# Two rounds of H3 and S4D long convolutions: rounded angles on ScalarE and VectorE, a folded factor 2 dt, and other DRAM layouts for spectra and y

## The chip, the core and the metric

The kernel runs on one core of one Trainium2 chip. Times are device microseconds of one launch. The engines are named as in the profile: PE is TensorE (PEld its weight loads), DVE is VectorE, ACT is ScalarE, POOL is GpSimd, SP is SyncE, which issues nearly all DMAs here. Each engine works through its own instructions in the order in which the program holds them; an instruction that waits holds back everything behind it on that engine.

## The reference, cut to what matters

```python
def _A_ref(q, k, v, shift_k, ssm_k, ssm_D):        # q is the normed x
    kv = k_shift * v                               # k_shift: short causal convolution of k
    y = irfft(rfft(kv) * rfft(ssm_k))[:S] + kv * ssm_D      # along 2048 positions, padded to 4096
    return q * y

def _B_ref(u, log_A_real, A_imag, C_real, C_imag, log_dt, D_skip):
    dt = exp(log_dt)
    A = -exp(log_A_real) + 1j * A_imag
    C = (C_real + 1j * C_imag) * dt[:, None]
    P = exp((A * dt[:, None])[:, :, None] * pos)   # 512 channels, 128 modes, 2048 positions
    K = 2.0 * einsum("dn,dnl->dl", C, P).real
    y = irfft(rfft(u) * rfft(K))[:L]
    return y + u * D_skip

x = x + _A_ref(_layernorm(x), k, v, shift_k, ssm_k, ssm_D)
x = x + _B_ref(_layernorm(x), ...)
x = x + _A_ref(_layernorm(x), k, v, shift_k, ssm_k, ssm_D)
x = x + _B_ref(_layernorm(x), ...)
```

x is 2048 x 512 in float32. A's convolution y doesn't depend on x, so it is computed once and used in both rounds. B's kernel K doesn't depend on x either.

## The kernel before, in words

**Layout.** A position is 16 times a partition number plus a row t: x is a tile of 128 partitions x 16 rows x 512 channels. A convolution along 4096 points is done by matmuls with DFT matrices in two steps, with a VectorE transpose of 32 x 32 blocks between them, for one quarter q of 128 channels at a time: `fwd_group` (matmuls into `pf` at L171, transposes into `zk` or `zu` at L191), `f2_chunk` (matmuls into `pu` at L196, eight chunks c per quarter), the product with the spectrum, the inverse matmuls into `pi` (L290), a transpose into `w` (L305) and matmuls into `po` (L311).

**Parameters.** The part behind L326 makes four numbers for each channel and mode: the rate of the angle, the phase of C, the decay, and log|C|. `split` stores them in DRAM as `rows_d`. It also makes `dt2`, which is 2 dt broadcast over partitions.

**B's kernel K.** `taps` makes it in 64 steps (16 groups gi of 32 channels, four steps k each). A step takes an exponential of the decay and log|C| (`mags`, tiles `m1`, `m2`), an angle in turns (`angles`, a matmul into the PSUM tile `pa`), cosine and sine of it (`waves`, into `tt`), products of both (`products`, into `xy` and back into `tt`), and small matmuls that sum over the modes (`contract`, into the PSUM tile `pk`). [...] Before, VectorE rounds the angle by adding and subtracting a large number, and a second matmul with minus the identity subtracts the rounded number inside PSUM:

```python
V.tensor_scalar(y, pa, MAGIC, MAGIC, op0=ALU.add, op1=ALU.subtract)      # L482
T.matmul(pa, minus, y, start=False, stop=True, skip_group_check=True)    # L483
```

ScalarE then reads `pa` three times for a step: the absolute value (L491), a sine of `pa` for the sine (L492) and a sine of the absolute value for the cosine (L493). After four steps of a group, two VectorE multiplications (L528, L529) bring `pk` times `dt2` into `ks`, which goes to DRAM (`kdram`). Exponentials and sines need different tables of ScalarE, so the twelve exponentials of two groups stand together.

**Spectra.** `spectrum_quarter` reads K (which = 1) or A's kernel (which = 0) from DRAM, transforms it, copies each chunk from PSUM to `pc` (L244) and stores that in `spec` (L245), a 256-KB chunk at a time. `convolution` loads the chunks as `kab` (L259), with one DMA for each half of the partitions. `pc` has two buffers.

**A's part.** `diagonal` computes the gated kv, A's spectrum, and `convolution(0)`, which copies its result from `po` to `ya` (L655) and stores it in `ya_d`, 16 tiles of 128 x 512. `gated_update` runs once in each round: it loads a quarter of the 16 rows of `ya_d` as `yaq` (L703; in the first round x too, at L701), forms (x + nm) * y in `ut` on one of three engines (L714, L717, L719, L720) and adds rs times that to x (L721).

**Order of the program.** `run_steps` interleaves the generators of taps (with B's spectrum at its end) and of A's part, one step to two. Within the bounds that the data set, a scheduler at build time puts the instructions of every engine in an order of its own, by times that it assumes. So a change in one place moves instructions in others. By the names, the program runs in this order: parameters, taps beside A's spectrum and gated kv, taps beside A's convolution, the first gated update beside the last taps, the norm and the end of B's spectrum, `conv_b(0)`, the second gated update, `conv_b(1)` with the stores of the result. Memory for x and for the tiles of the first gated update comes free when A's convolution is done.

Of the kernel before, what the change touches and what calls it, by code (L numbers as in the profile page):

```python
# [9 lines left out]
F32 = mybir.dt.float32  # L10
# [89 lines left out]
def kernel(ctx: ExitStack, tc: tile.TileContext, out, x_in, kv_in, ssmk_in, ssmd_in,  # L100
# [119 lines left out]
    def spectrum_quarter(which, q, src, pool, zlast, zb, tag):  # L220
# [18 lines left out]
        for c in range(NCH):  # L239
            pu, ins = f2_chunk(z, c, None, tag)  # L240
            if c == NCH - 1:
                zlast.append(ins)
            pc = pool.tile([128, CK * 128], F32, name="pc", tag="pc", bufs=2)
            S.copy(pc, pu.rearrange("p k c -> p (k c)"))  # L244
            nc.sync.dma_start(spec[which][q][c], pc)  # L245
            yield
# [3 lines left out]
    def convolution(which, pools, steps, finish, lag, ahead, nk, ns, nw, inplace, add_dve, zlast=None, late_step=None, first_b=False):  # L250
# [3 lines left out]
        def load(s):  # L254
            q, c = divmod(s, NCH)
            pool = pools["conv"]
            kab = pool.tile([128, 2, CK, 128], F32, name="kab", tag="kab", bufs=nk)
            for h in range(2):
                (G if first_b and s < GL else nc.sync).dma_start(kab[64 * h:64 * h + 64].rearrange("p r k c -> p r (k c)"),  # L259
                                  spec[which][q][c].rearrange("(r k) x -> k r x", r=2))  # L260
# [73 lines left out]
    G.memset(warm, 0.0)  # L334
    S.activation(warm, warm, AF.Exp)
    dt = gp.tile([128, 4], F32, name="dt")
    nc.sync.dma_start(dt, ldt_in)
    nc.sync.dma_start(flat(cr), cr_in)
# [7 lines left out]
    dt2 = gp.tile([128, NQ, 32], F32, name="dt2")  # L346
    halfpi = gp.tile([128, 1], F32, name="halfpi")
    G.memset(halfpi, math.pi / 2)

    minus = gp.tile([128, 128], F32R, name="minus")  # L350
    G.dma_start(minus, minus_in)

# [14 lines left out]
    across = lambda t_: t_[:, :, None].to_broadcast([128, 4, 128])  # L367
    S.activation(dt, dt, AF.Exp)
    S.activation(la, la, AF.Exp)
# [33 lines left out]
    V.scalar_tensor_tensor(t1, t3, 0.5, t1, op0=ALU.mult, op1=ALU.add)  # L403
    V.tensor_add(t2, t2, t1)

# [12 lines left out]
    S.activation(dt2, dt2, AF.Exp)  # L418
    V.tensor_scalar_mul(dt2, dt2, 2.0)
    nctx.close()  # L420
# [22 lines left out]
    rows, ms, xys, pks, angs = {}, {}, {}, {}, {}  # L443
    NXY = 2
    NM1 = 9
    NM2 = 5
# [27 lines left out]
    def angles(gi, k):  # L474
        h, s = divmod(k, 2)
        hs = slice(64 * h, 64 * h + 64)
        pa = pp.tile([128, 512], F32, name="pa", tag="pa", bufs=NPA)
        T.matmul(pa, rows[gi][hs, 0, :], tabs["tt"][hs, 8 * s:8 * s + 8, :], start=True, stop=False,
                 skip_group_check=True)

        y = wk.tile([128, 512], F32R, name="y", tag="y", bufs=2)
        V.tensor_scalar(y, pa, MAGIC, MAGIC, op0=ALU.add, op1=ALU.subtract)  # L482
        T.matmul(pa, minus, y, start=False, stop=True, skip_group_check=True)  # L483
        angs[gi, k] = pa

    def waves(gi, k):
# [4 lines left out]
        S.activation(co, rv, AF.Abs)  # L491
        for i in (S.activation(tt[:, 1, :, 1:65], rv, AF.Sin, scale=TWO_PI),  # L492
                  S.activation(co, co, AF.Sin, scale=-TWO_PI, bias=halfpi)):  # L493
            after(i, last_exp[0])
            last_sin[0] = i
# [15 lines left out]
    def contract(gi, k):  # L511
# [10 lines left out]
        if k < 3:  # L522
            return
        q, g = divmod(gi, 4)
        ks = wk.tile([128, 64, 8], F32, name="ks", tag="ks", bufs=2)
        d2 = dt2[:, q, 8 * g:8 * g + 8][:, :, None].to_broadcast([128, 8, 32])
        kv_ = ks.rearrange("p n c -> p c n")
        V.tensor_mul(kv_[:, :, 32:64], pk[:, :, 0:32], d2)  # L528
        V.tensor_mul(kv_[:, :, 31::-1], pk[:, :, 32:64], d2)  # L529
        for i4 in range(4):  # L530
# [58 lines left out]
    with ExitStack() as actx:  # L589
# [63 lines left out]
        def finish_a(q, g, po):  # L653
            ya = ap.tile([128, 512], F32, name="ya", tag="pc", bufs=2)
            S.copy(ya, po.rearrange("p t c -> p (t c)"))  # L655
            nc.sync.dma_start(ya_d[4 * q + g], ya)

# [39 lines left out]
    def gated_update(buffer, spare, rnd, load_x=False):  # L697
        yas = []
        for k in range(4):
            if load_x:  # L700
                nc.sync.dma_start(x[:, 4 * k:4 * k + 4, :], x_in[:, 4 * k:4 * k + 4, :])  # L701
            ya = buffer(k)
            nc.sync.dma_start(ya.rearrange("p g t c -> p g (t c)"),  # L703
                              ya_d[:, :, 128 * k:128 * k + 128].rearrange("g p x -> p g x"))
            yas.append(ya)
# [209 lines left out]
```

## Time and profile before

| | |
|---|---|
| median of three runs | 800.36 us (798.78 to 801.9) |
| profiled execution | 805.59 us |
| its span, first to last instruction | 803.8 us |
| mean granted clock of TensorE | 0.877 |
| busy: PE, DVE, POOL, ACT | 79%, 77%, 66%, 59% of the span |
| busy: weight loads of PE, beside its matmuls | 56% |
| moved by DMA | 135.47 MB, 169 GB/s on the mean |

The profile comes from one execution, whose time is 0.65% above the median; 1.8 us of it lie outside the span. A row of a group of instructions in it reads: source line, engine, operation, output and inputs by the program's names, shape, count, then busy time in us, mean ns of one instruction, and the idle time just before them with the instruction that ended most of it. No engine is full over the whole span, so the shares above are means over stages with different limits, and the stages have to be read one by one.

### The profile page before, as it was taken

The page shows a single profiled execution, that of the slowest core. Times are in us where ns is not written, and L with a number is a line of the kernel's source. Part 1 is how long each engine was busy: PE and PEld are TensorE (multiplying, and loading weights), DVE is VectorE, ACT ScalarE, POOL GpSimd, SP SyncE. Part 2 cuts the span into 40 slices and gives each one's busy share as a digit, 9 for nine tenths or more (in the row PEclk, how much of TensorE's full clock was granted, in tenths as well). Part 3 has the DMA queues.
Part 4 walks back from the last instruction along what each step waited for, and adds up shares of the span by engine and source line. Part 5 has one row for each costly group of instructions (what it writes and reads, how often), then busy time and mean ns, then how long its engine had stood idle before and what let it go on. Part 6 is the DMA issues. An engine that isn't in the chain of part 4 may idle for free. (4 is left out here: it accounts for less than half of the span.)

```text
span 803.8 us, 14448 instructions
## 1 busy us (share of the span) xinstructions
PE 635.2 (79%) x5064; PEld 447.3 (56%) x5064; DVE 621.3 (77%) x939; ACT 477.7 (59%) x879; POOL 533.7 (66%) x496
## 2 busy tenths in 40 slices
PE   3378696688799989999889863599789750998996
PEld 2255565356567747767556442386657620476673
DVE  7757979998967967647759499845668889878776
ACT  4035355345378875776785765649746525878573
POOL 4965778776778965838956277316665836288783
PEclk9676599868999999999899665789989995899999
DMA  9577177367477463664441593147987642068792
GB/s 326 188 247 270 40 241 254 108 200 254 146 215 203 127 182 110 182 171 123 115 131 34 174 341 105 46 129 199 233 200 183 159 103 54 1 164 223 201 252 105
DMA packets 89612, 135.47 MB, mean 169 GB/s; under 512 B 8508, under 2 KB 37700, under 8 KB 89028
## 3 DMA queue, kind: packets, MB, share of 16 engines
q1 hardware_dynamic: 88644, 132.13, 56.5%
q0 software_dynamic: 896, 2.43, 1.1%
q8 instruction: 40, 0.66, 0.4%
q14 instruction: 32, 0.26, 0.1%
HBM read 98.87 MB, written 35.65 MB: 167 GB/s over the span
## 5 line engine op out<-in xcount | busy, mean ns | idle before, releaser
L280 POOL TENSOR_TENSOR sw<-sw,kab 128x512 f32<-128x512 f32 x96 | 124.4, 1302 | 67.6 <-ACT sw L277 59.6
L196 PEld LDWEIGHTS pu<-zu,w 128*128 128x128 f32 x768 | 95.7, 193 | 52.9 <-DVE vv L278 18.6
L196 PE MATMUL pu<-zu,w 128*128 128x128 f32 x768 | 109.5, 285 | 15.1 <-DVE vv L278 12.8
L504 POOL TENSOR_TENSOR xy<-tt,m 128x512 f32<-128x512 f32 x64 | 84.9, 1327 | 53.5 <-ACT tt L493 23.8
L171 PE MATMUL pf<-kk,wz 128*128 128x256 f32 x256 | 86.3, 481 | 41.8 <-POOL kk L236 25.3
L278 DVE TENSOR_TENSOR vv<-pu,kab 128x512 f32<-128x512 f32 x96 | 64.9, 679 | 63.9 <-ACT sw L277 27.0
L290 PE MATMUL pi<-vv,mm 128*128 128x128 f32 x768 | 107.3, 285 | 3.5 <-DVE vv L278 2.6
L281 POOL TENSOR_TENSOR vv<-vv,sw 128x512 f32<-128x512 f32 x76 | 98.8, 1303 | 13.6 <-DVE vv L278 10.3
L290 PEld LDWEIGHTS pi<-vv,mm 128*128 128x128 f32 x768 | 96.5, 197 | 15.0 <-issue 9.1
L276 ACT ACTIVATE sw<-pu 64x512 f32<-64x512 f32 x96 | 57.0, 594 | 63.3 <-PE pu L196 60.8
L171 PEld LDWEIGHTS pf<-kk,wz 128*128 128x128 f32 x256 | 56.7, 237 | 62.3 <-POOL kk L236 33.3
L491 ACT ACTIVATE tt<-pa 128x512 f32<-128x512 f32 x64 | 38.3, 599 | 82.1 <-PE pa L483 72.3
L196 PE MATMUL pu<-zk,w 128*128 128x128 f32 x512 | 78.3, 307 | 6.4 <-DVE zk L191 4.2
L196 PEld LDWEIGHTS pu<-zk,w 128*128 128x128 f32 x512 | 72.7, 217 | 15.6 <-DVE zk L191 6.3
L505 DVE TENSOR_TENSOR tt<-tt,m 128x512 f32<-128x512 f32 x64 | 79.9, 1248 | 0.9 <-ACT tt L493 0.4
L244 ACT COPY pc<-pu 128x512 f32<-128x512 f32 x64 | 37.4, 591 | 57.3 <-PE pu L196 35.3
L506 DVE SCALAR_TENSOR_TENSOR xy<-tt,m 128x256 f32<-128x256 f32 x64 | 51.5, 805 | 25.7 <-ACT tt L492 15.3
L468 ACT ACTIVATE m<-pm 128x512 f32<-128x512 f32 x96 | 53.8, 604 | 22.6 <-PE pm L466 21.6
L483 PE MATMUL pa<-y,minus 128*128 128x512 f32 x64 | 37.1, 588 | 32.0 <-DVE y L482 30.5
L311 PE MATMUL po<-w,w 128*64 128x512 f32 x192 | 55.4, 655 | 7.3 <-DVE w L305 7.0
L519 PE MATMUL pk<-xy,tt 128*32 128x64 f32 x2048 | 50.5, 242 | 13.3 <-DVE ks L529 9.0
L519 PEld LDWEIGHTS pk<-xy,tt 128*32 128x32 f32 x2048 | 37.7, 122 | 39.1 <-issue 28.9
(139 smaller groups left out, 1295.4 us busy)
## 6 DMA issues: line engine op xcount, KB each, us to landing
kab<-spec SPq DMA_DIRECT2D x188, 256.0 KB, 4.0
spec<-pc SPq DMA_DIRECT2D x64, 256.0 KB, 2.7
kvt<-kv_in SPq DMA_DIRECT2D x16, 624.0 KB
yaq<-ya_d SPq DMA_DIRECT2D x8, 1024.0 KB, 10.6
kk<-ssmk_in SPq DMA_DIRECT2D x16, 256.0 KB, 2.9
kv_d<-u SPq DMA_DIRECT2D x16, 256.0 KB, 7.5
kdram<-ks SPq DMA_DIRECT2D x64, 64.0 KB, 1.8
kk<-kdram SPq DMA_DIRECT2D x16, 256.0 KB, 2.7
```

The source lines that it names most:

```text
L171: yield T.matmul(o, w, rhs, start=True, stop=True)
L196: ins = T.matmul(pu[:, i, :], w2[:, c * CK + i, :], z[:, :, c * CK + i, :], start=True, stop=True)
L276: S.mul(sw[0:64], pu[64:128], -1.0)
L278: V.tensor_mul(vv, pu, kabs[s][:, 0])
L280: (V if last else G).tensor_mul(sw, sw, kabs[s][:, 1])
L281: (V if last or s % add_dve == add_dve - 1 else G).tensor_add(vv, vv, sw)
L290: i1s[t] = T.matmul(pi[:, i, :], mm[:, c * CK + i, :], vvs[t][:, i, :], start=True, stop=True)
L311: ins = T.matmul(po[64 * a:64 * a + 64], w4, ws[g][:, :, 16 * a:16 * a + 16, :].rearrange("p x t r -> p t x r"), start=True, stop=True, ti ...
L468: i = S.activation(m, pm, AF.Exp)
L504: G.tensor_mul(xy[:, :, :, 32:64], tt[:, :, :, 1:33], m1[:, :, 32:64][:, None].to_broadcast([128, 2, 8, 32]))
L505: (G if (4 * gi + k) % E2P == E2P - 1 else V).tensor_mul(e2, e2, m2[:, None].to_broadcast([128, 2, 8, 32]))
L519: T.matmul(pk[32 * i4:32 * i4 + 32, 2 * k + i, :], e2[:, r, 4 * i + i4, :], xy[:, r, 4 * i + i4, :], start=r == 0, stop=r == 1, tile_posit ...
```

## The change

Five things are changed.

1. **Rounding.** ScalarE adds the large number (`magic`, a tile of one column) and writes the sum to `y` in SBUF, which rounds it; VectorE then computes (y - MAGIC) - pa into `y`. The matmul with minus the identity, and the matrix, are gone. `y` has the opposite sign, so the sine takes a scale of -2 pi. `waves` reads `y`, not `pa`.
2. **2 dt.** The logarithm of 2 dt is added to log|C| by four VectorE instructions in the parameter part. `dt2`, its load, its exponential and its doubling are gone, and `ks` is two plain copies of `pk`, one on VectorE and one on ScalarE.
3. **Spectrum in DRAM.** Its chunk is stored as 64 x 2 x 512, so that a partition of `kab` reads 4 KB in one piece; one DMA fills both halves of the partitions.
4. **y in DRAM.** `ya_d` is 4 x 128 x 16 x 128. The stores of `ya` write pieces of 512 B; a load of `yaq` reads 8 KB per partition in one piece, where before it read 16 pieces of 512 B.
5. **Buffers.** `pc` of B's last quarter takes the memory and the nine buffers of `m1`.

```diff
-    spec = [[dram.tile([NCH, 128, CK * 128], F32, name=f"spec{i}_{q}") for q in range(NQ)] for i in range(2)]
+    spec = [[dram.tile([NCH, 64, 2, CK * 128], F32, name=f"spec{i}_{q}") for q in range(NQ)] for i in range(2)]
-    ya_d = dram.tile([16, 128, 512], F32, name="ya_d")
+    ya_d = dram.tile([4, 128, 16, 128], F32, name="ya_d")
...
-            pc = pool.tile([128, CK * 128], F32, name="pc", tag="pc", bufs=2)
+            if which == 1 and q == NQ - 1:
+                pc = wk.tile([128, CK * 128], F32, name="pc", tag="m1", bufs=NM1)
+            else:
+                pc = pool.tile([128, CK * 128], F32, name="pc", tag="pc", bufs=2)
             S.copy(pc, pu.rearrange("p k c -> p (k c)"))
-            nc.sync.dma_start(spec[which][q][c], pc)
+            nc.sync.dma_start(spec[which][q][c].rearrange("k r x -> r k x"), pc)
...
-            for h in range(2):
-                (G if first_b and s < GL else nc.sync).dma_start(kab[64 * h:64 * h + 64].rearrange("p r k c -> p r (k c)"),
-                                  spec[which][q][c].rearrange("(r k) x -> k r x", r=2))
+            (G if first_b and s < GL else nc.sync).dma_start(
+                kab.rearrange("p r k c -> p (r k c)"),
+                spec[which][q][c].rearrange("k r x -> k (r x)")[None].to_broadcast([2, 64, 2 * CK * 128]))
...
+    magic = gp.tile([128, 1], F32, name="magic")
+    G.memset(magic, MAGIC)
...
-    V.tensor_add(t2, t2, t1)
+    V.tensor_scalar(ldt, ldt, math.log(2.0), None, op0=ALU.add)
+    for g in range(4):
+        V.scalar_tensor_tensor(t2[:, g], t2[:, g], ldt[:, g:g + 1], t1[:, g], op0=ALU.add, op1=ALU.add)
...
-    nc.sync.dma_start(flat(dt2), ldtb_in[:, None, :].to_broadcast([4, 32, 128]))
-    S.activation(dt2, dt2, AF.Exp)
-    V.tensor_scalar_mul(dt2, dt2, 2.0)
...
-        T.matmul(pa, rows[gi][hs, 0, :], tabs["tt"][hs, 8 * s:8 * s + 8, :], start=True, stop=False,
-                 skip_group_check=True)
-        y = wk.tile([128, 512], F32R, name="y", tag="y", bufs=2)
-        V.tensor_scalar(y, pa, MAGIC, MAGIC, op0=ALU.add, op1=ALU.subtract)
-        T.matmul(pa, minus, y, start=False, stop=True, skip_group_check=True)
-        angs[gi, k] = pa
+        T.matmul(pa, rows[gi][hs, 0, :], tabs["tt"][hs, 8 * s:8 * s + 8, :], start=True, stop=True)
+        y = wk.tile([128, 512], F32, name="y", tag="y", bufs=NY)
+        S.activation(y, pa, AF.Identity, bias=magic)
+        V.scalar_tensor_tensor(y, y, MAGIC, pa, op0=ALU.subtract, op1=ALU.subtract)
+        angs[gi, k] = y
...
-        V.tensor_mul(kv_[:, :, 32:64], pk[:, :, 0:32], d2)
-        V.tensor_mul(kv_[:, :, 31::-1], pk[:, :, 32:64], d2)
+        V.tensor_copy(kv_[:, :, 32:64], pk[:, :, 0:32])
+        S.copy(kv_[:, :, 31::-1], pk[:, :, 32:64])
...
-            nc.sync.dma_start(ya_d[4 * q + g], ya)
+            nc.sync.dma_start(ya_d[:, :, 4 * q + g].rearrange("k p x -> p k x"), ya.rearrange("p (k x) -> p k x", k=4))
...
-            nc.sync.dma_start(ya.rearrange("p g t c -> p g (t c)"),
-                              ya_d[:, :, 128 * k:128 * k + 128].rearrange("g p x -> p g x"))
+            nc.sync.dma_start(ya.rearrange("p g t c -> p (g t c)"), ya_d[k].rearrange("p g x -> p (g x)"))
```

The order on the engines moves with it, in three places that the prediction uses. The line numbers of the changed kernel are a few higher than those of before for the same statement (L482 becomes L486, L505 becomes L508, L506 becomes L509). The number at a tile's name only tells its instances apart.

The first place is VectorE where the first gated update begins. `ut` and `x` belong to that update, `y`, `tt`, `xy` and `ks` to the taps, `zk` to B's spectrum. Before:

```order
L714 SCALAR_TENSOR_TENSOR ut_4858<-x_4839,nm_111,yaq_4847 128x512
L714 SCALAR_TENSOR_TENSOR ut_4867<-x_4839,nm_111,yaq_4847 128x512
L721 SCALAR_TENSOR_TENSOR x_4839,mv_107<-ut_4858,rs_110,x_4839 128x512
L721 SCALAR_TENSOR_TENSOR x_4839,mv_107<-ut_4867,rs_110,x_4839 128x512
L506 SCALAR_TENSOR_TENSOR xy_4543<-tt1_225,m1_4386 128x8x32
L482 TENSOR_SCALAR y_4574<-pa_4572 128x512
L721 SCALAR_TENSOR_TENSOR x_4839,mv_107<-ut_4871,rs_110,x_4839 128x512
L482 TENSOR_SCALAR y_4610<-pa_4608 128x512
L505 TENSOR_TENSOR tt1_225<-tt1_225,m2_4382 128x16x32
```

And with the change, from the same first instruction of the update on:

```order
L714 SCALAR_TENSOR_TENSOR ut_4827<-x_4808,nm_111,yaq_4816 128x512
L714 SCALAR_TENSOR_TENSOR ut_4836<-x_4808,nm_111,yaq_4816 128x512
L529 COPY ks_4570<-pk_4442 128x8x32
L509 SCALAR_TENSOR_TENSOR xy_4615<-tt1_226,m1_4371 128x8x32
L486 SCALAR_TENSOR_TENSOR y_4609<-y_4609,pa_4607 128x512
L508 TENSOR_TENSOR tt1_226<-tt1_226,m2_4363 128x16x32
L721 SCALAR_TENSOR_TENSOR x_4808,mv_107<-ut_4827,rs_110,x_4808 128x512
L191 STREAM_TRANSPOSE zk_4693<-pf_4714 128x8x2x32
L721 SCALAR_TENSOR_TENSOR x_4808,mv_107<-ut_4836,rs_110,x_4808 128x512
L486 SCALAR_TENSOR_TENSOR y_4638<-y_4638,pa_4636 128x512
```

The update's first instruction stands further back among the taps: ahead of it stand 60 of the 64 `y` and 58 of the `tt` and `xy` before, and 62 and 61 with the change, and of the 64 `zk` transposes 56 before and 59 with it.

The second place is SP, around the first load of x, where A's last `ya` is stored. Before:

```order
L656 DMA ya_d_81<-ya_4072 128x512
L656 DMA ya_d_81<-ya_4078 128x512
L531 DMA kdram13_78<-ks_4445 32x4x128 x4
L694 DMA w1_4841<-w1_in 128x128
L701 DMA x_4839<-x_in 128x2048
L226 DMA kk_4738<-kdram13_78 128x512
L703 DMA yaq_4847<-ya_d_81 128x16x128
```

With the change:

```order
L657 DMA ya_d_81<-ya_4041 128x4x128
L657 DMA ya_d_81<-ya_4047 128x4x128
L249 DMA spec1_2_63<-pc_4426 2x64x512
L695 DMA w1_4810<-w1_in 128x128
L249 DMA spec1_2_63<-pc_4464 2x64x512
L702 DMA x_4808<-x_in 128x2048
L704 DMA yaq_4816<-ya_d_81 128x2048
```

The load of x now stands behind two stores of B's third spectrum, and the shapes of the stores and loads are the new ones.

The third place is PE, where the taps end and `conv_b(0)` begins: `pf` from `kk` and `pu` from `zk` are the last quarter of B's spectrum, `pf` from `u` is the first transform of the normed x. Before:

```order
L171 MATMUL pf_4763<-kk_4760,wz_103 128x16x8x2 x2
L171 MATMUL pf_4767<-kk_4760,wz_103 128x16x8x2 x2
L171 MATMUL pf_4968<-u_4950,wz_103 128x16x8x2 x2
L171 MATMUL pf_4972<-u_4950,wz_103 128x16x8x2 x2
L171 MATMUL pf_4981<-u_4950,wz_103 128x16x8x2 x2
L196 MATMUL pu_4771<-zk_4724,w2_104 128x128 x4
L196 MATMUL pu_4779<-zk_4724,w2_104 128x128 x4
```

With the change:

```order
L171 MATMUL pf_4732<-kk_4729,wz_103 128x16x8x2 x2
L171 MATMUL pf_4736<-kk_4729,wz_103 128x16x8x2 x2
L196 MATMUL pu_4740<-zk_4693,w2_104 128x128 x4
L196 MATMUL pu_4748<-zk_4693,w2_104 128x128 x4
L196 MATMUL pu_4756<-zk_4693,w2_104 128x128 x4
L196 MATMUL pu_4764<-zk_4693,w2_104 128x128 x4
L196 MATMUL pu_4772<-zk_4693,w2_104 128x128 x4
L171 MATMUL pf_4937<-u_4919,wz_103 128x16x8x2 x2
```

Five of the eight chunks of that spectrum have moved ahead of the first transform of x.

More of the change, by code (lines that the diff above doesn't have):

```diff
@@ L335 @@
     S.activation(warm, warm, AF.Exp)
+    magic = gp.tile([128, 1], F32, name="magic")
+    G.memset(magic, MAGIC)
     dt = gp.tile([128, 4], F32, name="dt")
-    nc.sync.dma_start(dt, ldt_in)
+    ldt = gp.tile([128, 4], F32, name="ldt")
+    nc.sync.dma_start(ldt, ldt_in)
     nc.sync.dma_start(flat(cr), cr_in)
@@ L367 @@
     across = lambda t_: t_[:, :, None].to_broadcast([128, 4, 128])
-    S.activation(dt, dt, AF.Exp)
+    S.activation(dt, ldt, AF.Exp)
     S.activation(la, la, AF.Exp)
@@ L444 @@
     NXY = 2
+    NY = 2
     NM1 = 9
@@ L491, in waves @@
         S.activation(co, rv, AF.Abs)
-        for i in (S.activation(tt[:, 1, :, 1:65], rv, AF.Sin, scale=TWO_PI),
+        for i in (S.activation(tt[:, 1, :, 1:65], rv, AF.Sin, scale=-TWO_PI),
                   S.activation(co, co, AF.Sin, scale=-TWO_PI, bias=halfpi)):
```

5 lines of the change are left out of this document (removed).

## The prediction

> **What bounds the kernel now.** No engine is full over the span, so I cut it at the places where the work changes and read the view of windows: length, busy time of each engine, granted clock, share of the DMA engines.
>
> ```profile
> core 0: us, PE busy (x) PEld busy (x) DVE busy (x) ACT busy (x) POOL busy (x), PEclk, DMA share, GB/s
> 0.00:230.00 230.00, 165.19 (x1308) 116.02 (x1309) 198.48 (x262) 99.29 (x169) 163.07 (x160) 0.82 0.64 208
> 230.00:468.00 238.00, 219.27 (x2068) 154.85 (x2066) 164.07 (x223) 174.80 (x303) 162.34 (x151) 0.93 0.52 149
> 468.00:523.00 55.00, 24.71 (x299) 16.40 (x298) 52.10 (x83) 31.41 (x70) 35.34 (x28) 0.66 0.48 143
> 523.00:545.00 22.00, 20.90 (x120) 18.15 (x121) 9.14 (x18) 10.42 (x22) 3.39 (x8) 0.89 0.43 136
> 545.00:657.00 112.00, 95.53 (x610) 68.40 (x609) 81.52 (x144) 69.11 (x129) 75.22 (x66) 0.95 0.72 177
> 657.00:700.00 43.00, 15.71 (x40) 6.53 (x40) 41.19 (x117) 25.92 (x66) 20.35 (x22) 0.68 0.25 60
> 700.00:804.00 104.00, 93.89 (x624) 66.90 (x624) 74.78 (x98) 66.73 (x123) 74.00 (x65) 0.99 0.67 183
> ```
>
> The stages are: 1, parameters and taps beside A's spectrum (VectorE 198.48 of 230, 86% full); 2, taps beside A's convolution (PE 219.27 of 238, 92%); 3, the first gated update (VectorE 52.10 of 55, 95%); 4, the change to B (PE); 5, `conv_b(0)` (PE 85%); 6, the second gated update (VectorE 96%); 7, `conv_b(1)` (PE 90%).
>
> The waits confirm it for the steps at hand. ScalarE waits for the matmul that goes, and for a buffer of `pc`:
>
> ```profile
> ACT tt L491 <- PE pa L483: 72.3, 30, 8.5
> ACT pc L244 <- DMA spec<-pc: 20.5, 7, 7.2
> ```
>
> These are total us, the number of waits and the longest. The first is no gain by itself: in stage 2 ScalarE has time, PE does not.
>
> The chain of waits (start, us, what) shows where transfers set the end:
>
> ```profile
> 531.88 4.26 DMA spec<-pc
> 536.85 2.97 DMA spec<-pc
> 576.99 7.38 DMA kab<-spec
> 714.39 4.78 DMA kab<-spec
> ```
>
> **The change part by part.** Durations come from the groups of instructions (count, busy us, mean ns, idle before).
>
> ```profile
> L483 PE MATMUL pa<-y,minus 128*128 128x512 f32 x64 | 37.1, 588 | 32.0 <-DVE y L482 30.5 <-DMA spec<-pc 1.3 <-ACT tt L491 0.2
> L482 DVE TENSOR_SCALAR y<-pa 128x512 fp32r<-128x512 f32 x64 | 42.3, 670 | 2.0 <-PE pa L478 2.0
> L278 DVE TENSOR_TENSOR vv<-pu,kab 128x512 f32<-128x512 f32 x96 | 64.9, 679 | 63.9 <-ACT sw L277 27.0 <-DMA kab<-spec 14.0 <-PE pm L466 6.8
> L491 ACT ACTIVATE tt<-pa 128x512 f32<-128x512 f32 x64 | 38.3, 599 | 82.1 <-PE pa L483 72.3 <-POOL kk L236 4.9 <-issue 2.1
> L493 ACT ACTIVATE tt<-tt,halfpi 128x512 f32<-128x512 f32 x64 | 46.5, 727 | 0.1
> L717 ACT ACTIVATE ut<-x,nm 128x512 f32<-128x512 f32 x13 | 9.0, 712 | 9.6 <-DVE var L209 7.4 <-DVE nm L208 2.2
> L400 ACT ACTIVATE t<-t 128x512 f32<-128x512 f32 x1 | 0.6, 630 | 0.0
> L418 ACT ACTIVATE dt<-dt 128x128 f32<-128x128 f32 x1 | 0.3, 309 | 2.6 <-DMA dt<-ldtb_in 2.6
> L528 DVE TENSOR_TENSOR ks<-pk,dt 128x256 f32<-128x256 f32 x16 | 10.0, 623 | 5.8 <-PE pk L519 5.6
> L529 DVE TENSOR_TENSOR ks<-pk,dt 128x256 f32<-128x256 f32 x16 | 10.4, 647 | 0.0
> L505 DVE TENSOR_TENSOR tt<-tt,m 128x512 f32<-128x512 f32 x64 | 79.9, 1248 | 0.9 <-ACT tt L493 0.4
> L506 DVE SCALAR_TENSOR_TENSOR xy<-tt,m 128x256 f32<-128x256 f32 x64 | 51.5, 805 | 25.7 <-ACT tt L492 15.3 <-issue 10.4
> L191 DVE STREAM_TRANSPOSE zk<-pf 128x512 f32<-128x512 f32 x64 | 44.4, 701 | 13.8 <-PE pf L171 13.7
> ```
>
> Prices first. The new VectorE instruction reads PSUM and SBUF as L278 does, 0.679 us beside the 0.670 of L482: VectorE neither gains nor loses by rounding. The new rounding on ScalarE is a pass from PSUM (0.599, L491) with a bias tile; L717 with one costs 0.712, L400 without one 0.630, so I take 0.599 + 0.08 = 0.68. It lies between 0.60 and L493's 0.727. The absolute value and the sine now read SBUF, 0.63 for 0.60 each. So ScalarE pays 0.74 us more per step. Its copy of 128x256 for `ks` I put at 0.42 us, between L418 (0.309, half as many elements) and L400 (0.630, twice as many).
>
> *Stage 1.* VectorE is full, and five groups' `ks` lie here; each loses one of its two instructions (0.65): 5 x 0.65 = 3.2 us. The four small additions to log|C| replace an addition and the doubling of `dt2`. I take **-3**. The new order of an angle, ScalarE ahead of VectorE, can make VectorE wait: with the 26 steps that the order has here at up to 0.3 us, bounds are +8 and -8.
>
> *Stage 2.* Of L483 alone, the same window holds
>
> ```profile
> 230.00:468.00 238.00, 17.73 (x33) 6.49 (x33) 0.93 0.52 149
> ```
>
> PE loses 17.73 us. By the order two more steps of taps come in; with some 2.5 us for them PE has about 204 us of work. ScalarE goes the other way: 174.8 + 35 steps x 0.74 (25.9) + two more steps' other passes (2 x 2.0) + nine copies for `ks` (3.8) = 208.5 us, which in 238 us is 88%. The fullest 20 us of ScalarE that this trace has are the first row here:
>
> ```profile
> 540.00:560.00 20.00, 18.03 (x123) 13.40 (x123) 9.82 (x15) 17.62 (x36) 10.21 (x8) 1.00 0.71 192
> 460.00:480.00 20.00, 13.70 (x106) 10.08 (x106) 16.18 (x18) 12.11 (x23) 13.48 (x12) 0.67 1.10 343
> 560.00:580.00 20.00, 16.88 (x116) 14.22 (x115) 12.96 (x18) 15.59 (x31) 16.16 (x16) 0.91 0.96 232
> ```
>
> 17.62 of 20 is 88% too. So the bound passes from PE to ScalarE, and I expect no gain from the matmul. What can be late at the stage's end is x:
>
> ```profile
> 451.65 0.59 ACT L655 COPY ya<-po 128x512 f32<-128x512 f32 x1
> 458.25 0.39 SPq L701 DMA_DIRECT2D x<-x_in  x1
> 461.71 1.28 ACT L492 ACT_TABLE_LOAD   x1
> ```
>
> The load of x (458.25) follows A's last `ya` copy (451.65), since x takes that memory. In the new order this copy stands on ScalarE behind twelve exponentials, the table load and four sines; before it stood ahead of most exponentials. And the load stands behind two stores of `spec` on SP. Most of that lies beside the three steps of taps that stand ahead now; I take **+3**. Bounds: -16, if the stage follows PE (204 / 0.921 = 221.4), and +46, if ScalarE can be no fuller than now (73.4%; 208.5 / 0.734 = 284).
>
> *Stage 3.* VectorE is 95% full, and has less left: 3 x 1.248 (L505) + 3 x 0.805 (L506) + 2 x 0.67 (`y`) + 3 x 0.701 (`zk`) + 2 x 0.65 (`ks`) = 10.9 us. The loads of `yaq` in larger pieces lie beside those of x. I take **-10**; bounds -15 (the second update, with no taps beside it, takes 43 us where this one takes 55, and some contention goes too) and -4 (part of the wait for x moves in here).
>
> *Stage 4.* In the chain above, the two stores of `spec` take 4.26 + 2.97 = 7.2 us because `pc` has two buffers. With nine for eight chunks no copy waits for a store. That goes, and what is late next is PE:
>
> ```profile
> 523.57 6.77 PE pf L171 x20
> ```
>
> PE is 95% busy here, but it then works in a stretch with five chunks' `pu` already done in the order, ahead of `pf` from `u`. I take **-9** (7.2 and some 2 of PE's work that moves beside stage 3); bounds -5 and -11.
>
> *Stage 5.* The wait of 7.38 us for `kab` falls where SP issues two loads of `yaq` for the second update between loads of `kab`:
>
> ```profile
> 566.78 1.22 SPq L259 DMA_DIRECT2D kab<-spec  x2
> 568.11 0.53 SPq L703 DMA_DIRECT2D yaq<-ya_d  x1
> 568.76 2.81 SPq L259 DMA_DIRECT2D kab<-spec  x2
> 571.67 0.54 SPq L703 DMA_DIRECT2D yaq<-ya_d  x1
> 572.56 5.71 SPq L259 DMA_DIRECT2D kab<-spec  x3
> ```
>
> The DMA engines are 0.96 busy there at 232 GB/s (third 20-us row), but at 343 GB/s at 1.10 in the second row, where x loads too. The transfers of small pieces hold the engines longer for the same bytes: `yaq` reads 512 B, `kab` 2 KB a piece, and both now read larger ones. I take 5 of the 7.38, and 1 for one issue of `kab` in place of two (1.22 us for two, first row): **-6**; bounds -1 and -10.
>
> By the Trainium skill ("DMA: Bandwidth & Descriptors", Specifications) a transfer is at line rate from 512 B on, so `yaq` would have been so before; 232 against 343 GB/s at a like share speaks against it here, though the two rows hold other mixes of transfers.
>
> *Stage 6* stays, VectorE's own work. *Stage 7:* some of the 4.78 us for `kab`, **-2**; bounds 0 and -5. The stores of `spec` and `ya` in smaller pieces have no cost in my sum: other chunks are computed meanwhile. If that cover fails, two `pc` buffers wait longer, some 7 us by the waits above.
>
> Sum: -3 + 3 - 10 - 9 - 6 + 0 - 2 = **-27**. The profiled execution took 805.59 us, span 803.8 and 1.8 around it; 778.6. The median of the runs is 800.36 / 805.59 = 0.9935 of it: 773.5, so **774**.
>
> **The rivals.**
>
> - *Stage 2 follows PE* (-16 for +3): sum -46, 755. For it: PE is the fullest engine there now. Against it: ScalarE would be at 208.5 of 222, 94%, which no row shows.
> - *ScalarE half bound:* it reaches a share midway between 73.4% and 88%, 81%; stage 2 takes 257, +19: sum -11, 789 (782 to 800). For it: ScalarE's angle now waits for VectorE in between, on engines that keep their order.
> - *The clock falls.* Where PE is less busy its granted clock is lower: 0.66 at 24.71 of 55, 0.99 at 93.89 of 104. If stage 2 falls from 0.93 to 0.82 (stage 1, where PE is 72% busy), 204 us become 231, and at PE's share of 92% 251: +13, sum -17, 783. Against it: the matmul that goes leaves PE at 86%. The Trainium skill ("TensorE: Matmul & The Clock Gate", What's actually happening) has the throttled clock as the default, which activity releases; that speaks for this case, and the two rows agree.
> - *Large pieces save nothing:* the pieces of 512 B are as fast as those of 8 KB, and the wait for `kab` stays but for the 1 us of issue: sum -22, 778. It is the case of the rule on 512 B above.
> - *Slower: ScalarE is the bound and gets no fuller than now.* Rounding on ScalarE puts 35 x 0.74 us into an engine that stands between PE, VectorE and the copies of `sw`, `pi` and `pc`; at 73.4% stage 2 takes 284, +46, sum +16, 816. It decides from a share of about 78%: 208.5 / 0.78 = 267 eats the other stages' 30 us. Against it: the 72.3 us for which ScalarE waits on L483 now end, since that matmul is gone.
>
> **How the numbers follow.** Chances: forecast 0.40 (its own range 763 to 785, from the bounds taken together), stage 2 by PE 0.12, ScalarE half bound 0.20, clock 0.07, large pieces 0.08, slower 0.13. About 0.5%, 4 us, is what a measurement of this kernel can tell from no change. Of the half-bound case a third, 0.07, lies above 796 and counts as the same; all other cases but the last are faster: 0.80, 0.07, 0.13. The range is 752 to 800: it leaves out the slower case and the tail of the deepest gain.
>
> **What would show it.** In the changed profile, stage 2 should end within 5 us of now's 238, ScalarE at 85% or more and PE at about 86%, with the waits of L491's successor on PE gone. The first update should take 45 us, no `pc` should wait for a store at the end of B's spectrum, and the wait for `kab` beside the loads of `yaq` should be under 3 us. I am wrong if the rounding on ScalarE costs over 0.73 us, if stage 1 moves by more than 8 us, or if ScalarE's share in stage 2 stays under 80%.

## The result, and the profile after

The changed kernel takes **1604.66 us** (median of 4 runs, 1604.07 to 1605.23) where the kernel before takes 801.13: a ratio of 1.997, 95% interval 1.989 to 2.006. The forecast was 774. It is twice as slow, which none of the rivals named.

The page of the changed kernel: busy shares, then granted clock, DMA and GB/s in 40 slices, the hardware queue, and the chain by lines.

```profile
PE 792.2 (49%) x5000; PEld 555.4 (35%) x5000; DVE 596.4 (37%) x926; ACT 529.5 (33%) x958; POOL 524.5 (33%) x494
...
PEclk8676676666676866776668556575656585666656
DMA  7443443221212211212262112212110101111112
...
q1 hardware_dynamic: 63548, 132.05, 23.4%
...
DMA kab<-spec 39%; DMA spec<-pc 13%; DMA out_dram<-yo 3%; DMA kk<-kdram 3%; PE pf L171 3%; DMA yaq<-ya_d 2%; PE pu L196 2%; DMA xt<-x_in 2%; PE po L315 1%; DMA u<-kv_d 1%; DVE x L721 1%; PE pi L294 1%; SPq L657 1%; PE pm L470 1%; DMA kk<-ssmk_in 1%
```

Every engine idles for half of the span or more. VectorE and GpSimd have about the busy time that they had, ScalarE some 52 us more, mostly by the new rounding passes (64 at 0.68 us) and its copies for `ks`. The chain is made of transfers, `kab` and `spec` above all, and yet the DMA engines are busy for a tenth or two of the later slices. In the page of before the same row of the queue is

```profile
q1 hardware_dynamic: 88644, 132.13, 56.5%
```

The bytes are equal, 132 MB. The share is of 16 engines over the span, so the packets took 0.565 x 16 x 803.8 = 7270 us of engine time before and 0.234 x 16 x 1603.5 = 6000 after. For the same bytes the DMA engines worked less in all, so the moving itself did not get slower; fewer packets move at a time. The busy time of PE rose from 635.2 to 792.2 with 64 matmuls fewer; its granted clock fell from 0.877 to 0.67 on the mean. That this follows from the transfers, and is not their cause, is shown by experiment 4 below, where the clock falls to 0.71 though nothing but the shape of a load is changed.

By stages, cut as before (columns as in the prediction):

```profile
core 0: us, PE busy (x) PEld busy (x) DVE busy (x) ACT busy (x) POOL busy (x), PEclk, DMA share, GB/s
0.00:328.00 328.00, 191.18 (x1346) 134.61 (x1346) 197.77 (x262) 125.73 (x213) 163.12 (x162) 0.71 0.44 146
328.00:815.00 487.00, 257.97 (x2111) 178.95 (x2114) 156.83 (x223) 204.91 (x349) 161.77 (x156) 0.69 0.23 78
815.00:852.00 37.00, 9.47 (x170) 6.90 (x159) 34.62 (x61) 20.94 (x47) 29.98 (x22) 0.59 0.43 141
852.00:907.00 55.00, 25.48 (x147) 20.07 (x147) 13.35 (x31) 25.10 (x58) 1.94 (x4) 0.75 0.16 61
907.00:1228.00 321.00, 139.19 (x580) 101.72 (x578) 79.53 (x138) 59.33 (x106) 70.77 (x64) 0.63 0.15 59
1228.00:1295.00 67.00, 22.41 (x72) 10.15 (x69) 43.12 (x122) 30.72 (x77) 23.27 (x24) 0.64 0.13 47
1295.00:1603.00 308.00, 146.49 (x600) 103.00 (x598) 71.14 (x94) 62.78 (x112) 73.66 (x65) 0.64 0.15 62
```

The three stages with a convolution (2, 5, 7) took 238, 112 and 104 us and take 487, 321 and 308. B's two take nearly the same, 32 chunks of `kab` in some 310 us: about 10 us a chunk, whatever else they do. The share of the DMA engines in them is 0.15, little over two of sixteen. SyncE's list says the same. In such a stretch the issue of one load lasts about 10 us, where two issues took 1.22 us before (start, us, what, count):

```profile
895.70 80.74 SPq L262 DMA_DIRECT2D kab<-spec  x8
```

Eight loads of `kab` in 80.74 us are 10.1 us each. Last, the waits (total us, number, longest) and two pieces of the chain (start, us, what):

```profile
DVE vv L282 <- DMA kab<-spec: 461.4, 59, 19.4
POOL sw L284 <- DMA kab<-spec: 364.5, 51, 11.5
ACT pc L248 <- DMA spec<-pc: 186.1, 34, 26.9
```

```profile
1063.57 152.56 DMA kab<-spec x5
...
1325.66 83.91 DMA kab<-spec x3
```

**The theory (A).** The trace records every packet, that is, every piece that a DMA is cut into. A 4-KB packet of `kab` takes 159 ns on the median, a 2-KB packet of `spec` 84. A chunk of `kab` is 128 packets; two engines need 64 x 0.159 = 10.2 us for it, which is the 10.1 seen. And the number of packets in flight (begun and not yet ended), sampled every 20 ns in the first convolution of B, is 2 nearly all the time; in stage 1, where A's spectrum is stored, it is 2 more than half of the time (counted from the trace, share of samples):

```text
kernel, stretch (us)             0-1   2-3   4-5   6-13  14 and more
before, 550 to 640               17%    3%    2%    10%   67%
changed, 910 to 1210              0%   96%    0%     1%    3%
before, 100 to 230               25%    4%    3%    18%   50%
changed, 100 to 320               3%   58%    4%    15%   19%
```

What the two slow transfers have in common is a first dimension of 2: the source of `kab` is 2 x 64 x 4 KB (one copy for each half of the partitions), the target of a store is 2 x 64 x 2 KB (r ahead of k). The theory is that a DMA runs on as many engines as its outermost dimension gives, here two. Rival B is that the layout of `spec`, or the larger pieces, are slow in DRAM. Rival C is that the new order of the angles, with the low clock, is the cause.

### The profile page after: what moved, and what is told of

It reads as the page before. It is cut to its first block, busy times and chain, and to the rows that moved or that the text cites. A ratio compares the mean times of both kernels' runs of the same rounds, so it can differ in the third digit from the quotient of the medians.

```text
span 1603.5 us, 14226 instructions
## 1 busy us (share of the span) xinstructions
PE 792.2 (49%) x5000; PEld 555.4 (35%) x5000; DVE 596.4 (37%) x926; ACT 529.5 (33%) x958; POOL 524.5 (33%) x494
## 4 chain that ended last, share of the span: by engine, by line
DMA 66%; PE 10%; DVE 8%; ACT 5%; issue 4%; SPq 4%; POOL 3%; DVEq 0%; POOLq 0%; ACTq 0%
DMA kab<-spec 39%; DMA spec<-pc 13%; DMA out_dram<-yo 3%; DMA kk<-kdram 3%; PE pf L171 3%; DMA yaq<-ya_d 2%; PE pu L196 2%; DMA xt<-x_in 2%; PE po L315 1%; DMA u<-kv_d 1%; DVE x L721 1%; PE pi L294 1%; SPq L657 1%; PE pm L470 1%; DMA kk<-ssmk_in 1%
## 5 line engine op out<-in xcount | busy, mean ns | idle before, releaser
L294 PE MATMUL pi<-vv,mm 128*128 128x128 f32 x768 | 157.7, 373 | 219.2 <-DVE vv L282 169.5
L294 PEld LDWEIGHTS pi<-vv,mm 128*128 128x128 f32 x768 | 142.6, 278 | 238.6 <-issue 108.4
L196 PE MATMUL pu<-zu,w 128*128 128x128 f32 x768 | 151.9, 357 | 105.4 <-DVE vv L282 105.3
L196 PEld LDWEIGHTS pu<-zu,w 128*128 128x128 f32 x768 | 135.1, 262 | 163.9 <-DVE vv L282 109.3
L171 PE MATMUL pf<-kk,wz 128*128 128x256 f32 x256 | 105.2, 566 | 116.1 <-POOL kk L236 86.7
L315 PE MATMUL po<-w,w 128*64 128x512 f32 x192 | 82.8, 965 | 78.6 <-DVE vv L282 63.6
L248 ACT COPY pc<-pu 128x512 f32<-128x512 f32 x64 | 37.3, 584 | 225.0 <-DMA spec<-pc 186.1
L295 ACT COPY ie<-pi 128x512 f32<-128x512 f32 x64 | 37.3, 583 | 224.2 <-PE pi L294 224.0
L508 DVE TENSOR_TENSOR tt<-tt,m 128x512 f32<-128x512 f32 x64 | 66.5, 1038 | 53.3 <-ACT tt L496 52.2
L470 PE MATMUL pm<-tg,rw 64*128 64x512 f32 x96 | 49.6, 580 | 63.0 <-ACT pc L248 58.0
L171 PE MATMUL pf<-u,wz 128*128 128x256 f32 x168 | 55.4, 470 | 30.5 <-DMA u<-kv_d 23.7
```

What stands on the lines that cost most here:

```text
L171: yield T.matmul(o, w, rhs, start=True, stop=True)
L196: ins = T.matmul(pu[:, i, :], w2[:, c * CK + i, :], z[:, :, c * CK + i, :], start=True, stop=True)
L294: i1s[t] = T.matmul(pi[:, i, :], mm[:, c * CK + i, :], vvs[t][:, i, :], start=True, stop=True)
L315: ins = T.matmul(po[64 * a:64 * a + 64], w4, ws[g][:, :, 16 * a:16 * a + 16, :].rearrange("p x t r -> p t x r"), start=True, stop=True, ti ...
L470: mt = T.matmul(pm, rows[gi][hs, 1, :], rhs, start=True, stop=True)
L508: (G if (4 * gi + k) % E2P == E2P - 1 else V).tensor_mul(e2, e2, m2[:, None].to_broadcast([128, 2, 8, 32]))
```

## The experiments

Each time is a median; the ratio behind it, with its 95% interval, is to the kernel before in the same comparison (799 to 802 us in all of them).

**1. The loads cut in halves.** From the changed kernel:

```diff
-            (G if first_b and s < GL else nc.sync).dma_start(
-                kab.rearrange("p r k c -> p (r k c)"),
-                spec[which][q][c].rearrange("k r x -> k (r x)")[None].to_broadcast([2, 64, 2 * CK * 128]))
+            for h in range(2):
+                (G if first_b and s < GL else nc.sync).dma_start(
+                    kab[64 * h:64 * h + 64].rearrange("p r k c -> p (r k c)"),
+                    spec[which][q][c].rearrange("k r x -> k (r x)"))
```

> The changed kernel, with the load of a kab chunk as two DMAs of 64 partitions x 4 KB in place of one DMA over a 2 x 64 x 4 KB source; layout, bytes and pieces in DRAM are the same. Theory A (a DMA whose source or target has an outermost dimension of 2 runs on two DMA engines only): the 96 loads of about 64 x 0.159 = 10.2 us each go back to all engines, and only the 64 stores of spec (64 x 0.084 = 5.4 us each, also 2 outermost) stay slow: 800 to 900 us. Rival B (the new layout of spec, or pieces of 4 KB, are slow in DRAM): no more than a few per cent better than the changed kernel, about 1550 to 1600 us. Rival C (the new order of angles and the low clock are the cause): about 1600 us.

953.3 us, 1.192 (1.185 to 1.200). The layout, the bytes and the 4-KB pieces have stayed and 650 us are gone, so B and C fall as causes of most of it. It is above the 900 of A's bound, so A had the cost of the stores too low; what is left is mostly the other transfer with a 2, for which ScalarE waits 141.4 us here and 15.9 in experiment 3:

```profile
ACT pc L248 <- DMA spec<-pc: 141.4, 35, 8.9
```

**2. The stores cut in halves**, the loads left as the change has them:

```diff
-            nc.sync.dma_start(spec[which][q][c].rearrange("k r x -> r k x"), pc)
+            for r in range(2):
+                nc.sync.dma_start(spec[which][q][c][:, r, :], pc[64 * r:64 * r + 64])
```

> The changed kernel, with the store of a pc chunk as two DMAs of 64 partitions, kab loaded as in the changed kernel. Theory A: the loads stay on two DMA engines, so each of the three convolutions takes at least 32 x 10.2 = 326 us where they took 238, 112 and 104: about 230 + 326 + 55 + 20 + 326 + 43 + 326 = 1326, 1250 to 1450 us. Rival B: about 1550 to 1600 us. Rival C: about 1600 us.

1441.49 us, 1.805 (1.794 to 1.817), at the upper end of A's range. The loads alone keep most of the loss.

**3. Both cut in halves.**

> The changed kernel with both as two DMAs of 64 partitions: loads and stores have 64 as their outermost dimension. Theory A: what is left is the rest of the change as it was forecast, 763 to 785 us, with some more for 64 further issues of stores. Rival B: about 1600 us. Rival C: about 1600 us.

808.86 us, 1.013 (1.005 to 1.020). All of the factor of two is in these two statements. What is left of the change is not a gain of 3%, though, but a loss of 1.3%; experiments 5 to 11 take it apart.

**4. The fault alone, in the kernel before.** Old layout, old pieces, old number of DMAs; the two DMAs of a chunk are cut by rows instead of by halves of the partitions, which puts the 2 outermost:

```diff
-            for h in range(2):
-                (G if first_b and s < GL else nc.sync).dma_start(kab[64 * h:64 * h + 64].rearrange("p r k c -> p r (k c)"),
-                                  spec[which][q][c].rearrange("(r k) x -> k r x", r=2))
+            for r in range(2):
+                (G if first_b and s < GL else nc.sync).dma_start(kab[:, r].rearrange("p k c -> p (k c)"),
+                                  spec[which][q][c][64 * r:64 * r + 64][None].to_broadcast([2, 64, CK * 128]))
```

> The kernel before, with nothing of the change in it; only the two DMAs of a kab chunk are cut in another way: by the two rows r (128 partitions each, source 2 x 64 x 2 KB with the 2 outermost, read twice) in place of by the halves of the partitions (64 x 2 x 2 KB). Layout, bytes, pieces of 2 KB and the number of DMAs are those of before. Theory A: each DMA takes 64 x 0.084 = 5.4 us on two engines, a chunk 10.8, each convolution at least 344 us: about 1380, 1300 to 1480 us. Rival B: about 800 us. Rival C: about 800 us.

1462.65 us, 1.831 (1.820 to 1.842). With nothing of the change in it, the kernel before becomes as slow as the changed one with its stores mended (1441). Its windows in B's two convolutions:

```profile
750.00:1050.00 300.00, 118.99 (x512) 89.00 (x512) 63.56 (x108) 57.90 (x104) 61.45 (x57) 0.64 0.17 60
1150.00:1430.00 280.00, 122.05 (x511) 87.95 (x511) 58.45 (x78) 55.04 (x99) 60.37 (x56) 0.64 0.15 58
```

58 to 60 GB/s at a share of 0.15 to 0.17, as in the changed kernel (59 and 62 at 0.15).

**12 and 13. Four in place of two.** Two questions are open after that: whether the outermost dimension sets the number of engines in general, and whether it isn't the double read of one source that is slow. Both kernels load a chunk of the kernel before with four DMAs of 64 partitions x 2 KB; number 12 has 64 outermost, number 13 a gap in DRAM after every 16 rows, so that 4 stand outermost and no source is read twice by one DMA:

```diff
-    spec = [[dram.tile([NCH, 128, CK * 128], F32, name=f"spec{i}_{q}") for q in range(NQ)] for i in range(2)]
+    spec = [[dram.tile([NCH, 8, 17, CK * 128], F32, name=f"spec{i}_{q}") for q in range(NQ)] for i in range(2)]
...
+            for h in range(2):
+                for r in range(2):
+                    (G if first_b and s < GL else nc.sync).dma_start(
+                        kab[64 * h:64 * h + 64, r].rearrange("p k c -> p (k c)"), spec[which][q][c][4 * r:4 * r + 4, :16])
```

(Number 12 reads `spec[which][q][c][64 * r:64 * r + 64]`, of the old layout.)

> The kernel before with a kab chunk loaded by four DMAs of 64 partitions x 2 KB (half of the partitions, row r) in place of two; every one has 64 as its outermost dimension. The control of the next run. Theory A: all engines take part, what it costs is twice the issues on SP: 800 to 840 us. Rival L (cutting kab into other DMAs is what is slow): far over 900 us.

> As the run before, but spec in DRAM has a gap after every 16 rows (8 x 17 x 512, the 17th unused), so that each of the four DMAs reads 4 x 16 x 2 KB with 4 outermost, and a store of pc writes 8 x 16 x 2 KB. No source is read twice by one DMA. Theory A (the engines are as many as the outermost dimension): a DMA takes 16 x 0.084 = 1.35 us on four engines, a chunk 5.4 us, a convolution at least 172 us: B's two take 60 and 70 us longer than before, A's is hidden, so 920 to 990 us. Rival M (only a double read by one DMA is slow): as the run before, 800 to 840 us. Rival L: as the run before.

Number 12: 794.07 us, 0.990 (0.986 to 0.994); number 13: 1002.38 us, 1.249 (1.244 to 1.254). The cutting costs nothing, it even gains 1% and falls below the 800 to 840 that were expected; 4 outermost lie between 2 and 64, and rivals L and M are out. Number 13 is a little over A's range: A's convolution, which I took for hidden, became longer as well (stage 2 by some 45 us). Its stores of `pc` have changed too, to 8 outermost; what share they have in the 45 us isn't shown. B's two convolutions, which hold none of these stores, in number 13, and a stretch of the first in number 12:

```profile
599.00:767.00 168.00, 106.23 (x536) 79.11 (x536) 66.03 (x112) 62.08 (x113) 67.77 (x62) 0.77 0.33 112
829.00:983.00 154.00, 104.66 (x556) 75.00 (x556) 61.93 (x86) 59.60 (x107) 68.35 (x61) 0.82 0.29 113
```

```profile
550.00:630.00 80.00, 73.80 (x504) 57.43 (x504) 61.76 (x105) 53.16 (x97) 59.96 (x55) 0.96 0.78 212
```

168 us for 32 chunks, where four engines at 16 x 0.084 x 4 = 5.4 us a chunk need 172 less what is loaded ahead. The rates read 60, 113 and 212 GB/s for 2, 4 and 64 outermost; at 64 PE is 92% busy, so the transfers set the time no longer. The packets in flight:

```text
kernel, stretch (us)             0-1   2-3   4-5   6-13  14 and more
4 outermost, 900 to 980           0%    0%   90%     5%    5%
64 outermost, 550 to 630          3%    3%    4%    40%   50%
```

The Trainium skill states the rule ("DMA: Bandwidth & Descriptors", Why a DMA increments its semaphore by 16 and not by 1): a DMA takes the largest number of engines, up to 16, that divides the slowest dimension over 1 of both of its access patterns. The runs agree for 2 (a load that reads its source twice, and a store) and for 4 (a load with no double read). For a DMA of a hardware queue, as nearly all here are, the same section names the lowest-numbered engines; that several such loads, issued one behind the other, have two packets in flight together fits it, though the trace doesn't name the engine of a packet.

**5. The change with the old layout of `spec`.** Its store and loads are those of the kernel before, the other four parts those of the change.

> Everything of the change but the spectrum's layout: spec, its store and the two loads of a kab chunk as in the kernel before. The kernel with both layouts' DMAs cut in halves took 808.9 us. Theory D (there the 128 stores of 128 KB delay the end of B's spectrum, its stage 4 is 7 us longer than before): those 7 us go, about 800 us or a little less. Rival E (the other parts of the change cost what is left): 805 to 812 us. The forecast on record, less the 2 us it gave to fewer issues and larger pieces of kab: about 776 us.

801.09 us, 1.001 (0.996 to 1.005), as D in the expectation has it: the loss left in experiment 3 belongs to the layout of `spec` with its further stores. The other four parts together give nothing, where the forecast gave them 25 us.

**6 to 9. Each of the four alone**, put into the kernel before. The edits are those of the diff of the change.

> The kernel before with the rounding alone changed (ScalarE adds, VectorE subtracts, no matmul with minus the identity). Forecast's steps: nothing in stage 1, +3 in stage 2, some of the -10 in stage 3: 793 to 800 us. Rival F (the angle's way through ScalarE first makes VectorE wait in stage 1, as the bound of +8 had it): 804 to 810 us, the loss before the first product of A's convolution.

> The kernel before with 2 dt folded into log|C| alone. Forecast's steps: 3 us less in stage 1 and 1 to 3 in the others, 793 to 797 us. Rival G (the four additions take 1.3 us each on VectorE, where one took 1.1, and they lie ahead of the first taps; the copies of ks on ScalarE take 0.64 us): 798 to 805 us.

> The kernel before with the layout of y in DRAM alone changed (stores in pieces of 512 B, loads of 8 KB per partition in one piece). Forecast's steps: 5 us less where kab waits behind the loads of yaq: 793 to 796 us. Rival H (pieces save nothing there, and the stores now write pieces of 512 B): 799 to 803 us.

> The kernel before with pc of B's last quarter in the nine buffers of m1 alone. Forecast's step: the 7.2 us of waits for stores of spec in the chain go, 791 to 795 us. Rival I (those stores have to be done all the same before the next tiles take that memory, so PE and the stores follow at once): within 3 us of before, 797 to 802 us.

| part alone | us | ratio to before | interval | forecast, us |
|---|---|---|---|---|
| 6: rounding | 808.39 | 1.007 | 1.003 to 1.010 | 793 to 800 |
| 7: 2 dt folded | 797.38 | 0.993 | 0.989 to 0.996 | 793 to 797 |
| 8: layout of y | 804.18 | 1.001 | 0.997 to 1.005 | 793 to 796 |
| 9: buffers of `pc` | 802.61 | 1.000 | 0.996 to 1.003 | 791 to 795 |

The rounding costs 0.7%, inside the range of rival F; in its profile the first product of A's convolution comes 237 us after the start, where it came after 232. The folded factor gives it back, and the two that were to help transfers change nothing. Why, is told below.

**10 and 11.** The layout of `spec` alone, loaded and stored in halves as in experiment 3, and the two transfer parts together:

> The kernel before with the new layout of spec alone, loaded and stored by DMAs of 64 partitions, so that 64 is outermost everywhere: 4-KB pieces of kab, 64 further stores. Theory D (more stores to issue on SP delay the ends of the spectra): 803 to 810 us. Rival K (larger pieces gain as much as the issues cost): 794 to 801 us.

> The kernel before with the two parts that touch neither taps nor spectrum layout: y in the new layout, and pc of the last quarter in nine buffers. If their gains add and are those of the forecast: 786 to 791 us. If both rivals H and I hold: 797 to 802 us.

809.67 us, 1.012 (1.004 to 1.019), and 801.70 us, 0.998 (0.994 to 1.001). The five parts alone add to +0.7 - 0.75 + 0.1 + 0 + 1.15 = 1.2%, and experiment 3, which has them all, has 1.3%: the parts add up. Number 10 lies in D's range: the larger pieces of `kab` don't pay for the layout. ScalarE waits 32.9 us for stores of `pc` in it, for 20.5 before, which fits, but that it is the further stores that cost was not tried apart.

**14. The three parts that lost nothing alone:** 2 dt folded, y in the new layout, `pc` in nine buffers; rounding and layout of `spec` as before.

> The kernel before with 2 dt folded into log|C|, y in the new layout, and pc of the last quarter in nine buffers; rounding and the layout of spec as before. If the three add as they measured alone (797.4, 804.2 and 802.6 beside 802; the last two together 801.7): 795 to 799 us. Rival (the order that the build finds decides within 1%): 792 to 805 us.

794.58 us, 0.987 (0.982 to 0.992), 1.3% faster than the kernel before. That y and `pc` add to it isn't shown: 2 dt alone gave 0.993 (0.989 to 0.996), which overlaps, and of the 12 us between the two profiled executions 11 are there at the end of stage 2 (457 us for 468), ahead of the places that those two were to help.

## Why the prediction was wrong, step by step

**The step that failed** is in stage 5: "1 for one issue of `kab` in place of two", with the sentence on the stores in stage 7, "The stores of `spec` and `ya` in smaller pieces have no cost in my sum: other chunks are computed meanwhile." I priced a DMA by its bytes, its pieces and its issues, and took it as given that it spreads over all engines as the old ones did. So the loads stood in the sum as a gain, and the stores at nothing, with 7 us should the cover fail. The shape was before my eyes: an order row of the change reads `2x64x512` for the store, the diff broadcasts a source of 64 to 2 x 64. The trace of before doesn't show the rule on the engines; with it, and the packet times of that trace (4096 B 159 ns, 2048 B 85 ns on the median), two engines give 10.2 us a chunk, against 112 / 32 = 3.5 us of stage 5. In its place stands +800 us: the mended kernel of experiment 3 differs by 1604.66 - 808.86 = 796. The loads alone take 1604.66 - 953.3 = 651 of it, the stores alone 1604.66 - 1441.49 = 163. The cover of the stores failed: ScalarE waits 186.1 us for them, and the first product of A's convolution comes 328 us after the start (322 in experiment 1, 252 in experiment 2).

Two of the three signs of being wrong did show, and neither from ScalarE's price: stage 1 moved by 98 us, and ScalarE's share in stage 2 was 42%. The rounding on ScalarE took 0.68 us, as forecast.

The steps for the rest of the change, read from the mended runs:

*Stage 1, -3.* With both transfers mended (experiment 3) the first product of A's convolution comes 240 us after the start where it came after 232. This is the bound of +8 and not the value. One cost can be seen: the four additions to log|C|, which I put level with what they replace, took 1.3 us each there, VectorE's list:

```profile
24.35 5.02 DVE L412 SCALAR_TENSOR_TENSOR t<-t,ldt,t 128x128 f32<-128x128 f32 x4
```

In experiment 7, at another place among VectorE's instructions, they took 0.685 each; why isn't shown. They don't make the 8 us: in experiment 5 they took 1.3 as well and the first product comes after 236, in experiment 6, which hasn't got them, after 237. How the 8 us divide I can't say.

*Stage 2, +3, ScalarE as the new bound.* The size was near (+2 and -6 here), the picture not quite right. Stage 2 of experiment 6 (rounding alone) and of experiment 5:

```profile
237.00:477.00 240.00, 210.25 (x2021) 152.45 (x2021) 166.04 (x221) 195.37 (x335) 163.11 (x150) 0.92 0.51 146
```

```profile
236.00:468.00 232.00, 199.20 (x1982) 143.18 (x1981) 157.43 (x211) 195.71 (x339) 163.90 (x152) 0.96 0.55 159
```

PE lost its matmuls and the stage kept its length, 240 and 232 for 238: removing work from the fullest engine gave nothing, as forecast. But ScalarE stands at 81% and 84%, not at 88%, and PE at 88% and 86%; neither is full. ScalarE's work was overpriced in sum (some 196 us, not 208.5), for 34 and 32 steps of taps fell into the stage, not 35; the rounding itself was 0.68 as I had put it, and the copy for `ks` took 0.64 where I had put 0.42. What holds the stage at these shares may be the way of an angle through four engines in turn; no run shows it. Rounding alone costs 0.7% where I had it nearly free.

*Stage 3, -10.* In the changed kernel the stage takes 37 us for 55, and the work that was to go is gone from it: VectorE has 3 `tt`, 3 `xy` and 2 `y` there, before 6, 6 and 5. The mended kernels have an order of their own, with 6, 6 and 5 or 6 again. Their first update still takes 43 us (experiment 3) and 44 (experiment 5), from its first `ut` to its last instruction, for 49 before. That gain has another source: before, one of the first two `ut` took 6.8 us, VectorE's list:

```profile
468.50 7.44 DVE L714 SCALAR_TENSOR_TENSOR ut<-x,nm,yaq 128x512 f32<-128x512 f32 x2
```

In experiments 3 and 5 the two took 1.40 us, and an `xy` just ahead of the update took 5.3 us; what makes one instruction so long isn't shown. So the size that came near the forecast was luck. And the gain doesn't reach the end: stages 3 and 4 together take 77 us before and in experiment 5, and 81 in experiment 3.

*Stage 4, -9 for the buffers of `pc`.* Wrong: alone they give 0 (0.996 to 1.003). The chain of experiment 9 (start, us, what) at that place:

```profile
520.72 6.57 PE pf L171 x20
527.28 1.79 PE pu L196 x16
529.07 2.59 PE pf L171 x12
531.66 1.79 PE pu L196 x16
533.45 1.73 PE pf L171 x8
535.18 4.52 PE pu L196 x40
539.69 1.06 PE pf L171 x4
540.75 1.98 PE pu L196 x16
542.74 1.08 PE pf L171 x4
```

The two waits for `spec` are gone from it, and PE works without a gap from 520.7 to 543.8. It had nearly done so before, at 95% of the stage: the waits stood in the chain, but PE had other work to do beside them. In PE's list of before the one gap from 523.6 to 547.6 is the 0.54 us at the end of this row:

```profile
540.55 2.05 PE L196 MATMUL pu<-zk,w 128*128 128x128 f32 x16 [0.54 <-ACT pc L244]
```

I had written the 95% and credited the 7.2 us all the same.

*Stage 5, -6 for larger pieces of `yaq`.* Wrong: alone they give 0.1% (-0.3 to +0.5). In experiment 8 the load in 8-KB pieces takes 10.0 us to land, in 512-B pieces 10.6 before and 8.5 in experiment 10; and the wait for `kab` is still there, 13.76 us in the chain for 7.38 (issues with KB and median us to landing; a piece of the chain):

```profile
yaq<-ya_d SPq DMA_DIRECT2D x8, 1024.0 KB, 10.0
```

```profile
570.44 13.76 DMA kab<-spec
```

The size of the pieces changes next to nothing: the rival "large pieces save nothing" is the one that holds, and with it the line of the Trainium skill ("DMA: Bandwidth & Descriptors", Specifications) that 512 B is enough for line rate, which the prediction had set aside for two rows with other mixes of transfers. The larger pieces of `kab` bring no more: a load of 256 KB lands in 4.0 us in 2-KB pieces (before) and in 4.0 in 4-KB pieces (experiment 3).

*2 dt, -4 in all:* right, -0.75%, some 6 us, though where the gain arises isn't shown: in its profile the first product of A's convolution comes after 235 us, no earlier than before.

The rival that ended slower rested on ScalarE and would have given 816. The clock did fall to 0.67, but as a consequence of waits, and it was 0.868 with the mended DMAs. That the kernel became slower, as that rival had it, has another cause.

## What to carry to other kernels

Price a DMA by the number of engines that it can use, ahead of its bytes, pieces and issues: read the outermost dimension of source and target, and where it is 2 (a broadcast to two halves, a swapped axis), multiply the time of one packet by half of the packets and compare that with the stage. A low share of the DMA engines beside long waits for DMAs was the mark of it in this profile. And before a wait in the chain is credited, look whether the engine that it feeds, or another on the same way, is full anyway: in stage 4 that engine kept the time.

## What the runs showed that I had not expected

Four loads of 128 KB for a chunk in place of two of 256 KB, with 64 outermost, made the kernel 1.0% faster (0.986 to 0.994), though SyncE issues twice as many of them; why is open. Of the 12 us between the two profiled executions 6 are there at the first product of A's convolution (226 us for 232). Four VectorE operations of 128x128 took 1.31 us each in one place of the program and 0.68 in another. And with the transfers on two engines TensorE's granted clock was 0.63 to 0.64 in B's convolutions, where it had been 0.95 to 0.99: PE's work in stage 5, 96 us before, became 139.
